# Cached attention on one Trainium2 core: K's transpose in two halves, the first wq on ScalarE's queue, K and V in whole transfers

## The chip, the cores and the metric

The kernel runs on one core of a Trainium2 chip. The metric is the time of one execution on the device in microseconds (us); the median of three runs stands for a kernel. A core has TensorE (PE, matrix products; its weight loads are shown apart as PEld), VectorE (DVE), ScalarE (ACT), GpSimd (POOL) and SyncE (SP), each with a program of its own. They meet through semaphores only. Transfers between the chip's main memory and the on-chip memory are issued by an engine and carried out by DMA engines. TensorE writes to eight banks of an accumulator memory called `ps` here.

## What is computed

Two independent attention blocks, A and B, whose results stand side by side in the output. For each:

```python
B, Sq, D = 16, 64, 640          # x: [B, Sq, D]
H, Sk, Dh = 32, 512, 128        # k_cache, v_cache: [B, H, Sk, Dh]
q = (x @ wq).reshape(B, Sq, H, Dh).transpose(0, 2, 1, 3)
scores = einsum("bhqd,bhkd->bhqk", q, k_cache) * Dh ** -0.5
p = softmax(scores, axis=-1)
o = einsum("bhqk,bhkd->bhqd", p, v_cache)
out = o.transpose(0, 2, 1, 3).reshape(B, Sq, H * Dh) @ wo
```

All inputs and the output are bf16. K and V are read once and are nearly all of the bytes.

## The kernel before

**Tiling.** The unit of work is a *pack* n: two batch rows (2 x 64 queries) and four heads. There are 128 packs. Four packs in a row (j = 0 to 3) share the two batch rows and make a group; eight groups make a phase, which uses one part of wq and wo (16 heads). Two phases do block A, two do block B. A pack needs 1 MB of K and 1 MB of V.

**Steps of a pack**, by the names that the plan uses:

- QP (L688): TensorE projects x to q, 20 matmuls. QE (L694): ScalarE copies q out of `ps`, scaled.
- KT (L702): VectorE transposes the pack's K, `kn_ring` to `kt_ring`, in one instruction of 128 x 2048 values of 4 bytes (pairs of bf16).
- S (L712): TensorE makes the scores, 32 matmuls in four accumulation steps f = 0 to 3. The steps f = 0, 1 read the half of K's transpose with index j = 0 in `kt_ring`, f = 2, 3 the half with j = 1.
- EX (L741): ScalarE takes the exponential of each of the four heads and its row sums; RC (L754): VectorE takes reciprocals, two heads at a time; NM (L762): GpSimd normalises P.
- TR (L774): TensorE transposes P; TE (L854): VectorE copies transposed P out of `ps`, in two instructions.
- PV (L867): TensorE multiplies P with V; OE (L875), ZO (L879): ScalarE copies the result out and clears the bank.
- OP (L887): TensorE multiplies with wo, accumulating over four packs; OS (L897, L900): VectorE adds the groups of two phases.

Beside these, per group: XT (L662), XE (L668), XS (L672), XC (L677) transpose and place x. Per phase: WP (L656), eight copies by GpSimd, permutes wq from `ws_sb`, where it lands, to `wqp_sb`, where QP reads it. A WP of pack 0 needs all five parts of wq (LDWQ, 512 KB each, in rows of 4 KB).

**Order.** `build_plan` writes out the order. Each step has a time in packs in the table `AT`; the program of each compute engine is its steps sorted by n plus that time. So TensorE runs S(n), TR(n-1), OP(n-2), QP(n+1), PV(n-1), S(n+1), and VectorE runs KT(n+1), TE(n-1), RC(n), KT(n+2). Before S(0) TensorE runs QP(0) and a dummy PV on zeros, n = -2. VectorE begins with memsets (VZ, BZ, WZ). TensorE's program and ScalarE's are loops of four packs; the first turn's instructions have to be brought in as it runs.

**Transfers.** SyncE issues nearly all of them, on one queue, in the order of a second key: LDWQ of the first phase at -50, then LDK(n), LDX, LDV(n) and LDWO by due time. At the start this gives five LDWQ, K(0), K(1), K(2), x of group 1, V(0), wo, K(3), V(1), wo, K(4), V(2) and so on. ScalarE's queue has one transfer, the first x. `kn_ring` holds six packs of K, `v_ring` four of V, `kt_ring` two transposes. LDV(n) may be issued when PV(n-4) is done, for which SyncE waits for TR(n-3). For packs below `KSPLIT` = 8, K comes in four transfers of 256 KB (L629) and V in two of 512 KB (L646); after that K comes in two of 512 KB (L631) and V in one of 1 MB (L641), but for the last two packs, whose V is cut otherwise (L648).

**Waits.** `stand_in` replaces a wait on a step by one on a later step that implies it, and `order_waits` drops those already implied. A step's wait for V or wo may stand with an earlier step of another engine.

Of the kernel before, what the change touches and what calls it, by code (L numbers as in the profile page):

```python
# [6 lines left out]
F32 = mybir.dt.float32  # L7
# [13 lines left out]
class Cfg:  # L21
    NK = 6
    NV = 4
    NKT = 2
# [5 lines left out]
    PERIOD = 4  # L30
    BASE = 32
    KLEAD = 2.5
    KSPLIT = 8
    NARROW = 2
    AFTER = 24
    AT = dict(XT=-2.585, XE=-2.383, XS=-1.65, XC=-0.788, QP=-0.428, QE=-0.224, KT=-0.672, S=0,
              EX=(0.307, 0.252, 0.358, 0.4), RC=(0.45, 0.6), RCO=0.48, NM=(0.803, 0.854, 1.088, 1.187),
              RCZ=(0.475, 0.6), NMZ=(0.48, 0.49, 0.61, 0.62), TR=1.293, TE=(1.432, 1.47), PV=1.701, OE=(1.888, 2.013), ZO=2.221,
              OP=2.387, OS=2.576, LDWO=2.6, ST=2.8,
# [47 lines left out]
def build_plan(dims, cfg, general):  # L87
# [4 lines left out]
    NPH, NBP, NJ = dims["NPH"], dims["NBP"], dims["NJ"]  # L92
    PH = NBP * NJ
    N = NPH * PH
    AT = cfg.AT
    ops = []
    loads = []
    at = {}

    def add(eng, kind, idx, ts, reads=(), writes=()):  # L100
        op = Op(eng, kind, idx, ts, reads, writes)
        ops.append(op)
        at[(kind, idx)] = op
        return op

    def add_output(n):
        g, j = n // NJ, n % NJ
        final = n >= 0 and dims["FINAL"](g // NBP)
        apart = 0 <= n < cfg.KSPLIT or n >= N - cfg.NARROW
        for b in range(0 if apart else 1, 2):  # L110
# [61 lines left out]
    for ph in range(NPH):  # L172
        twp = [ph * PH + t for t in AT["WP1" if ph else "WP0"]]
        for kt in range(dims["KT"]):
            ready = (twp[-1] - PH if ph > 1 else AT["WP0"][-1]) + 0.5
            op = add("sp", "LDWQ", (ph, kt), twp[0] - 0.5 if ph else -20.0, [], [("ws", kt, j) for j in range(NJ)])
            loads.append((ready + 2.0 + 0.14 * PH * kt if ph > 1 else AT["PV"] + 0.15 if ph else -50.0, 1, op))
        for j in range(NJ):
            w = ph * NJ + j
            n0 = ph * PH + j  # L180
            for i in range(2):
                add("pool", "WP", (w, i), twp[2 * j + i], [("ws", kt, j) for kt in range(dims["KT"])], [("wqp", j, i)])
            if ph:
                loads.append((n0 - NJ + AT["LDWO"], 4, add("sp", "LDWO", w, n0 + AT["OP"] - 0.8 * NJ, [], [("wo", j)])))
            else:
                loads.append((n0 - 1.9, 4, add("sp", "LDWO", w, n0 + AT["OP"] - 0.8 * NJ, [], [("wo", j)])))
# [6 lines left out]
    for n in range(-2, N):  # L193
        add_output(n)
        if n < 0:
            continue
        g, j = n // NJ, n % NJ
        add("pe", "QP", n, n + AT["QP"], [("xT", g % cfg.NX), ("wqp", j, 0), ("wqp", j, 1)], [("SB", 1)])
        add("act", "QE", n, n + AT["QE"], [], [("SB", 1), ("qs", n % cfg.NQ)])
        for i in range(4):  # L200
            if i < 2 or n < cfg.KSPLIT:
                op = add("sp", "LDK", (n, i), n + AT["KT"] - 0.9, [], [("kn", n % cfg.NK)])
                loads.append((n - cfg.NV + AT["PV"] + 0.2 - cfg.KLEAD, 2, op))
        add("dve", "KT", n, n + AT["KT"], [("kn", n % cfg.NK)], [("kt", n % cfg.NKT)])
        add("pe", "S", n, n + AT["S"], [("qs", n % cfg.NQ), ("kt", n % cfg.NKT)],
            [("SB", i) for i in range(4)])
        for i in range(4):
            h = 4 * n + i
            te = n + AT["EX"][i]
            if general:  # L210
                add("dve", "MX", h, te - 0.002, [], [("SB", i), ("negmax", h % 4)])
            add("act", "EX", h, te, [("negmax", h % 4)] if general else [],
                [("SB", i), ("pn", n % cfg.NPN, i), ("rs", n % cfg.NRS, i)])
            add("pool" if n < N - 1 else "dve", "NM", h, n + (AT["NM"] if n < N - 1 else AT["NMZ"])[i],
                [("recip", n, i // 2)], [("pn", n % cfg.NPN, i)])
        for a in range(2):
            add("dve", "RC", (n, a), n + (AT["RCZ"][a] if n == N - 1 else AT["RCO"] if n % NJ == 1 and not a else AT["RC"][a]), [("rs", n % cfg.NRS, i) for i in (2 * a, 2 * a + 1)],
                [("recip", n, a)])
# [62 lines left out]
    def stand_in(d, op):  # L281
        if op.eng == "pe":
            if d.kind == "XE":
                return at[("QE", max(0, NJ * d.idx - 2))]
            if d.kind == "NM" and d.eng == "pool":
                return at[("NM", d.idx | 3)]
            if d.kind == "OE":
                return d if d.idx[1] == 0 else at[("ZO", d.idx[0])]
            if d.kind in ("EX", "MX") and not for_pe(d):
                if op.kind == "S":  # L290
                    return at[("QE", op.idx)]
                return d if id(op) not in inside and d.kind == "EX" else None
            return d
        if d.kind == "PV" and op.eng == "sp":
            return at[("TR", d.idx + 1)]
        if d.kind == "QP" and op.eng == "pool":
            return at[("TR", d.idx - 1)]
        if d.kind == "XT" and op.eng == "sp":
            return at[("XE", d.idx)]
        if d.kind == "OS" and op.eng == "sp" and for_pe(d):  # L300
            return at[("RC", (d.idx * NJ + NJ + 1, 1))]
        if not for_pe(d):
            return d
        if d.kind == "NM":
            return at[("TR", d.idx // 4)]
        if d.kind == "KT":
            return at[("S", d.idx)]
        if d.kind == "EX":
            alt = at[("EX", d.idx // 4 * 4)]
            return at[("EX", d.idx // 4 * 4 + 2)] if for_pe(alt) else alt  # L310
        if d.kind == "OS":
            return at[("PV", d.idx * NJ + NJ)]
        if d.kind == "TE":
            return at[("PV", d.idx[0])]
        if d.kind == "OE":
            return at[("OP", d.idx[0])]
        if d.kind == "QE":
            return at[("S", d.idx)]
        if d.kind == "XC":
            return at[("QP", d.idx * NJ)]  # L320
        raise RuntimeError(f"no stand-in for {d.kind} before {op.kind}")
# [2 lines left out]
    counts = dict(base)  # L324

    def sem_key(op):
        if op.kind == "LDX" and op.eng == "act":
            return ("d_first",) + op.writes[0]
        if op.kind == "LDV":
            return ("d_v" if op.idx[1] else "d_vh", op.writes[0][1])  # L330
        if op.kind in LOADS:
            return ("d_" + op.kind[2:].lower(),) + op.writes[0][1:]
        if op.kind in ("ST", "STH"):
            return ("d_out",)
        return ("q_" + op.eng,) if for_pe(op) else ("s_" + op.kind.lower() + "_" + op.eng,)
# [169 lines left out]
def mha_kernel(nc, blocks, out, cfg=None):  # L505
    cfg = cfg or Cfg()
# [4 lines left out]
    KT = D // 128  # L511
    scale = float(DH) ** -0.5
    assert D // 2 + 128 <= 512
    NBP, NJ = B // 2, 4
# [15 lines left out]
    NK, NV, NKT, NX, NXN, NQ, NPN, NRS = (cfg.NK, cfg.NV, cfg.NKT, cfg.NX, cfg.NXN, cfg.NQ, cfg.NPN, cfg.NRS)  # L530

    with contextlib.ExitStack() as es:
# [8 lines left out]
        kn_ring = sb("kn_ring", [128, NK, 2, 2048], BF16)  # L541
        kt_ring = sb("kt_ring", [128, NKT, 32, 2, 2, 16, 2], BF16)
# [81 lines left out]
        def em_LDK(e, op):  # L624
            n, b, l = op.idx[0], op.idx[1] // 2, op.idx[1] % 2
            blk, bp, j, h = pack_info(n)
            src = blocks[blk][1][2 * bp:2 * bp + 2, h:h + 4].rearrange("b h (p l t) d -> l (h p) b (t d)", l=2, t=32)[l]
            if n < cfg.KSPLIT:
                ins = e.dma_start(kn_ring[2 * b + l::4, n % NK].rearrange("p a c -> p (a c)"), src[:, b])  # L629
# [66 lines left out]
            return ins, ins  # L696

        def em_KT(e, op):
            n = op.idx
            dst = kt_ring[:, n % NKT].rearrange("p t j b k two -> p (t j) b (k two)").bitcast(F32)  # L700
            src = kn_ring[:, n % NK].rearrange("p a c -> p (a c)").bitcast(F32).rearrange("p (c h b l) -> p c h b l", h=8, b=2, l=2)
            ins = e.transpose(dst.rearrange("p c b (h l) -> p c h b l", h=8, l=2), src)  # L702
            return ins, ins

        def em_S(e, op):
            n = op.idx
            first = last = None
            for f in range(4):
                for b in range(2):
                    for i in range(4):  # L710
                        rows = slice(32 * i, 32 * i + 32)
                        last = e.matmul(ps[64 * b:64 * b + 64, i, :], qs_ring[rows, n % NQ, f, b, :],  # L712
                                        kt_ring[rows, n % NKT, :, f // 2, b, :, f % 2],
                                        start=(f == 0), stop=(f == 3), tile_position=(32 * i, 64 * b))
                        first = first or last
            return first, last
# [354 lines left out]
```

## Time and profile before

The three runs took 731.67, 732.18 and 732.88 us, a median of 732.18. All views are of one profiled execution:

| what | value |
|---|---|
| time of the profiled execution | 732.12 us |
| its span, first to last instruction | 730.4 us |
| mean granted clock of TensorE | 0.99 |
| bytes moved by DMA | 295.02 MB, mean 404 GB/s |
| chain that ended last, shares | PE 53%, DMA 32%, SP's queue 6%, DVE 3% |
| VectorE's wait for K, both blocks | 120.4 us |
| TensorE's first projection | 15.48 us |

In the page's lists a row names line, engine, operation and tiles, then count, busy time, mean of one, and the idle time just before it with what ended it. In the 40 slices each digit is a share in tenths. The timeline gives start, duration, engine, line and tile, and in brackets how long the engine sat idle before it and for whom. A trailing q at an engine's name (SPq, ACTq) stands for its queue of transfers. "issue" marks idle time of an engine for which the profile shows no other engine or transfer as the reason.

### The profile page before, as it was taken

To read this page: it belongs to the slowest core of one execution; us is meant where nothing else is said; L and a number is where in the kernel's file an instruction comes from. 1 tells how busy PE (TensorE), PEld (TensorE's weight loads), DVE (VectorE), ACT (ScalarE), POOL (GpSimd) and SP (SyncE) were. 2 spreads that over 40 slices of the span, in tenths; PEclk is the share of its full clock that TensorE was granted. 3 is DMA by queue.
4 is the path that set the end of the run, shared out by engine and by line. 5 is a ranking of instruction groups with operands and counts; after the bars stand their busy time and mean duration, and the time that the engine had idled before them with its cause. 6 is when DMAs were issued, how large, how long until landed. Compare 5 with 4: busy or idle time off the path is not lost.

```text
span 730.4 us, 61195 instructions
## 1 busy us (share of the span) xinstructions
PE 674.1 (92%) x28502; PEld 530.3 (73%) x28502; DVE 514.5 (70%) x691; ACT 533.3 (73%) x1574; POOL 417.9 (57%) x596
## 2 busy tenths in 40 slices
PE   1679999999999999999997899999999799999998
PEld 1458778787777777777775677787777577787775
DVE  5447777777777766767765667677777567878775
ACT  1447878778787777777875677777778677878775
POOL 4436565666875455554884555465587446555552
PEclk9889999999999999999999999999999999999999
DMA  8999999999999999999999999999999999999993
GB/s 337 401 404 414 414 415 413 415 414 415 415 400 409 419 414 416 416 416 417 416 411 402 415 414 413 414 415 415 414 416 407 403 415 418 417 418 417 416 415 122
DMA packets 72336, 295.02 MB, mean 404 GB/s; under 512 B 7664, under 2 KB 20080, under 8 KB 55920
## 3 DMA queue, kind: packets, MB, share of 16 engines
q1 hardware_dynamic: 72160, 294.52, 100.0%
q8 instruction: 10, 0.16, 0.1%
q10 hardware_dynamic: 144, 0.16, 0.1%
q14 instruction: 22, 0.18, 0.1%
HBM read 292.03 MB, written 2.62 MB: 403 GB/s over the span
## 4 chain that ended last, share of the span: by engine, by line
PE 53%; DMA 32%; SPq 6%; DVE 3%; issue 3%; POOL 2%; ACT 1%; DVEq 0%; POOLq 0%
DMA xn_ring<-in_B_x_dram 14%; PE ps L867 12%; PE ps L887 11%; PE ps L688 11%; PE ps L712 10%; DMA kn_ring<-in_A_k_cache_dram 9%; PE ps L774 7%; DMA kn_ring<-in_B_k_cache_dram 5%; DMA wo_sb<-in_B_wo_dram 4%; SPq L631 4%; DVE kt_ring L702 2%; POOL pn_ring L762 2%; SPq L641 1%; DVE pT_sb L854 1%; SPq L615 1%
## 5 line engine op out<-in xcount | busy, mean ns | idle before, releaser
L762 POOL TENSOR_SCALAR pn_ring<-pn_ring,recip 128x512 bf16<-128x512 bf16 x508 | 343.4, 695 | 246.1 <-DVE recip L754 221.0
L702 DVE STREAM_TRANSPOSE kt_ring<-kn_ring 128x2048 f32<-128x2048 f32 x128 | 295.3, 2307 | 120.3 <-DMA kn_ring<-in_B_k_cache_dram 80.3
L741 ACT ACTIVATE pn_ring<-ps 128x512 bf16<-128x512 f32 x512 | 296.4, 592 | 5.7 <-PE ps L712 5.7
L854 DVE COPY pT_sb<-ps 128x1024 bf16<-128x1024 bf16 x256 | 168.4, 671 | 60.2 <-PE ps L774 60.2
L688 PE MATMUL ps<-xT_ring,wqp_sb 128*128 128x128 bf16 x2560 | 165.9, 220 | 11.6 <-POOL xT_ring L677 11.6
L867 PE MATMUL ps<-pT_sb,v_ring 32*128 32x64 bf16 x16448 | 162.2, 192 | 10.6 <-DVE pT_sb L854 4.6
L688 PEld LDWEIGHTS ps<-xT_ring,wqp_sb 128*128 128x128 bf16 x2560 | 157.5, 114 | 17.8 <-issue 11.8
L867 PEld LDWEIGHTS ps<-pT_sb,v_ring 32*128 32x128 bf16 x16448 | 147.0, 91 | 24.8 <-issue 12.5
L887 PE MATMUL ps<-wo_sb,oT_sb 128*128 128x320 bf16 x1024 | 163.5, 303 | 0.0
L875 ACT ACTIVATE oT_sb<-ps 128x256 bf16<-128x256 f32 x257 | 84.7, 381 | 95.1 <-PE ps L867 95.1
L712 PE MATMUL ps<-kt_ring,qs_ring 32*64 32x512 bf16 x4096 | 138.4, 380 | 4.8 <-issue 4.8
L694 ACT ACTIVATE qs_ring<-ps 128x512 bf16<-128x512 f32 x128 | 76.4, 597 | 76.5 <-PE ps L688 74.5
L774 PEld LDWEIGHTS ps<-ident,pn_ring 64*128 64x128 bf16 x4096 | 68.3, 95 | 77.0 <-ACT oT_sb L875 46.0
L887 PEld LDWEIGHTS ps<-wo_sb,oT_sb 128*128 128x128 bf16 x1024 | 90.4, 98 | 36.7
L741 ACT ACTIVATION_READ_ACCUMULATOR pn_ring<-ps 128x1 f32 x512 | 105.3, 206 | 0.0
L774 PE MATMUL ps<-ident,pn_ring 64*128 64x64 bf16 x4096 | 82.9, 191 | 22.8 <-POOL pn_ring L762 18.6
L712 PEld LDWEIGHTS ps<-kt_ring,qs_ring 32*64 32x64 bf16 x4096 | 53.4, 103 | 32.9 <-issue 5.5
L754 DVE RECIPROCAL recip<-rowsum 128x2 f32<-128x2 f32 x256 | 40.6, 158 | 27.6 <-ACT pn_ring L741 24.6
L879 ACT ACTIVATE ps<-zeros 128x256 f32<-128x256 bf16 x128 | 49.5, 387 | 4.1
L656 POOL COPY wqp_sb<-ws_sb 128x1280 bf16<-128x1280 bf16 x32 | 39.6, 1256 | 9.9 <-DMA ws_sb<-in_A_wq_dram 6.8
L668 ACT ACTIVATE xe_sb<-ps 128x640 bf16<-128x640 bf16 x32 | 22.9, 716 | 8.7 <-PE ps L662 8.6
L677 POOL COPY xT_ring<-xe_sb 128x640 bf16<-128x640 bf16 x16 | 11.5, 717 | 21.0 <-PE ps L774 21.0
(42 smaller groups left out, 103.5 us busy)
## 6 DMA issues: line engine op xcount, KB each, us to landing
kn_ring<-in_B_k_cache_dram SPq DMA_DIRECT2D x128, 512.0 KB, 16.1
v_ring<-in_B_v_cache_dram SPq DMA_DIRECT2D x62, 1024.0 KB, 16.5
kn_ring<-in_A_k_cache_dram SPq DMA_DIRECT2D x112, 512.0 KB, 11.4
v_ring<-in_A_v_cache_dram SPq DMA_DIRECT2D x56, 1024.0 KB, 14.8
kn_ring<-in_A_k_cache_dram SPq DMA_DIRECT2D x32, 256.0 KB, 8.6
v_ring<-in_A_v_cache_dram SPq DMA_DIRECT2D x16, 512.0 KB, 8.9
ws_sb<-in_A_wq_dram SPq DMA_DIRECT2D x10, 512.0 KB, 9.3
wo_sb<-in_A_wo_dram SPq DMA_DIRECT2D x8, 640.0 KB, 13.3
```

The costliest lines, as they stand in the source:

```text
L688: last = e.matmul(ps[:, 1, f * 128:(f + 1) * 128], w[:, kt, f, :], xT_ring[:, xs, kt, :], start=(kt == 0), stop=(kt == KT - 1))
L694: ins = e.activation(qs_ring[:, op.idx % NQ].rearrange("p f b q -> p (f b q)"), ps[:, 1, :], ACTF.Copy, scale=scale)
L702: ins = e.transpose(dst.rearrange("p c b (h l) -> p c h b l", h=8, l=2), src)
L712: last = e.matmul(ps[64 * b:64 * b + 64, i, :], qs_ring[rows, n % NQ, f, b, :], kt_ring[rows, n % NKT, :, f // 2, b, :, f % 2], start=(f = ...
L741: ins = e.activation(dst, src, ACTF.Exp, scale=1.0, accum_out=sum_of(h))
L762: ins = e.tensor_scalar(pn_view(h), pn_view(h), recip[:, h:h + 1], 1.0, ALU.mult, ALU.mult)
L774: last = e.transpose(pt_bank(b)[:, 64 * c:64 * c + 64], pn[rows, c, :], ident[rows, rows], tile_position=(64 * b, 0))
L854: ins = e.tensor_copy(pT_sb[:, b].rearrange("p t q -> p (t q)"), pt_bank(b))
L867: last = e.matmul(ps[:, 4 + i, 64 * b:64 * b + 64], v_ring[rows, n % NV, b, c, :], pT_sb[rows, b, c, :], start=(t == 0 and i < 2), stop=(t ...
L875: ins = e.activation(oT_sb[:, 2 * a:2 * a + 2, :], o_ps[:, 2 * a:2 * a + 2, :], ACTF.Copy)
L879: ins = e.activation(z_ps, zeros[:, :].unsqueeze(2).broadcast_to([128, 2, 128]), ACTF.Copy)
L887: last = e.matmul(out_ps[:, s, :], oT_sb[:, i, :], wo_sb[:, 4 * j + i, s * NH0:(s + 1) * NH0], start=(j == 0 and i == 0), stop=(j == NJ - ...
```

## The change

Three things are changed.

K's transpose and the scores are each made in two halves. `KT` becomes (n, 0) and (n, 1), each 128 x 1024 values; the second is placed at n - 0.39, which on VectorE is behind TE of pack n - 2 and the second RC of pack n - 1. The scores become S (f = 0, 1), which waits for the first half, and SL (f = 2, 3), which waits for the second and stands right behind S. The stand-ins for KT and QE become SL.

The first phase's five LDWQ are issued by ScalarE behind its load of x, with semaphores of their own (`d_first`); SyncE's queue begins with K(0).

`KSPLIT` becomes 0: K and V of the first eight packs come in the same transfers as those of later packs.

```diff
-    KSPLIT = 8
+    KSPLIT = 0
-    AT = dict(XT=-2.585, XE=-2.383, XS=-1.65, XC=-0.788, QP=-0.428, QE=-0.224, KT=-0.672, S=0,
+    AT = dict(XT=-2.585, XE=-2.383, XS=-1.65, XC=-0.788, QP=-0.428, QE=-0.224, KT=(-0.672, -0.39), SL=0.1, S=0,
...
-            op = add("sp", "LDWQ", (ph, kt), twp[0] - 0.5 if ph else -20.0, [], [("ws", kt, j) for j in range(NJ)])
-            loads.append((ready + 2.0 + 0.14 * PH * kt if ph > 1 else AT["PV"] + 0.15 if ph else -50.0, 1, op))
+            op = add("sp" if ph else "act", "LDWQ", (ph, kt), twp[0] - 0.5 if ph else -20.0 + 0.1 * kt, [],
+                     [("ws", kt, j) for j in range(NJ)])
+            if ph:
+                loads.append((ready + 2.0 + 0.14 * PH * kt if ph > 1 else AT["PV"] + 0.15, 1, op))
...
-                op = add("sp", "LDK", (n, i), n + AT["KT"] - 0.9, [], [("kn", n % cfg.NK)])
+                op = add("sp", "LDK", (n, i), n + AT["KT"][0] - 0.9, [], [("kn", n % cfg.NK)])
...
-        add("dve", "KT", n, n + AT["KT"], [("kn", n % cfg.NK)], [("kt", n % cfg.NKT)])
-        add("pe", "S", n, n + AT["S"], [("qs", n % cfg.NQ), ("kt", n % cfg.NKT)],
-            [("SB", i) for i in range(4)])
+        for a in range(2):
+            add("dve", "KT", (n, a), n + AT["KT"][a], [("kn", n % cfg.NK)], [("kt", n % cfg.NKT, a)])
+        add("pe", "S", n, n + AT["S"], [("qs", n % cfg.NQ), ("kt", n % cfg.NKT, 0)], [("SB", i) for i in range(4)])
+        add("pe", "SL", n, n + AT["SL"], [("qs", n % cfg.NQ), ("kt", n % cfg.NKT, 1)], [("SB", i) for i in range(4)])
...
-            return at[("S", d.idx)]
+            return at[("SL", d.idx[0])]
...
-            return at[("S", d.idx)]
+            return at[("SL", d.idx)]
...
-        if op.kind == "LDX" and op.eng == "act":
+        if op.kind in ("LDX", "LDWQ") and op.eng == "act":
...
-            n = op.idx
-            dst = kt_ring[:, n % NKT].rearrange("p t j b k two -> p (t j) b (k two)").bitcast(F32)
-            src = kn_ring[:, n % NK].rearrange("p a c -> p (a c)").bitcast(F32).rearrange("p (c h b l) -> p c h b l", h=8, b=2, l=2)
-            ins = e.transpose(dst.rearrange("p c b (h l) -> p c h b l", h=8, l=2), src)
+            n, a = op.idx
+            dst = kt_ring[:, n % NKT, :, a].rearrange("p t b k two -> p t b (k two)").bitcast(F32)
+            src = kn_ring[:, n % NK].rearrange("p a c -> p (a c)").bitcast(F32)
+            src = src.rearrange("p (t j h b l) -> p j t h b l", j=2, h=8, b=2, l=2)[:, a]
+            ins = e.transpose(dst.rearrange("p t b (h l) -> p t h b l", h=8, l=2), src)
             return ins, ins
 
         def em_S(e, op):
-            n = op.idx
+            return scores(e, op.idx, 0)
+
+        def em_SL(e, op):
+            return scores(e, op.idx, 2)
+
+        def scores(e, n, low):
             first = last = None
-            for f in range(4):
+            for f in range(low, low + 2):
```

## The prediction

> **What bounds the kernel now.** I read the page first (busy shares, the 40 slices, the chain), then cut the start into 1 us and 4 us windows, then the timeline of the start and of the end, and last what SyncE's queue waits for.
>
> ```profile
> span 730.4 us, 61195 instructions
> PE 674.1 (92%) x28502; PEld 530.3 (73%) x28502; DVE 514.5 (70%) x691; ACT 533.3 (73%) x1574; POOL 417.9 (57%) x596
> DMA  8999999999999999999999999999999999999993
> GB/s 337 401 404 414 414 415 413 415 414 415 415 400 409 419 414 416 416 416 417 416 411 402 415 414 413 414 415 415 414 416 407 403 415 418 417 418 417 416 415 122
> DMA packets 72336, 295.02 MB, mean 404 GB/s; under 512 B 7664, under 2 KB 20080, under 8 KB 55920
> L702 DVE STREAM_TRANSPOSE kt_ring<-kn_ring 128x2048 f32<-128x2048 f32 x128 | 295.3, 2307 | 120.3 <-DMA kn_ring<-in_B_k_cache_dram 80.3
> ```
>
> No engine is the bound, the transfers are: 295.02 MB at the 415 GB/s of the middle slices are 711 us of 730.4, and DMA share stays at 9 up to the last slice. Only the first slice (337 GB/s) and the last have room. TensorE is close behind. Where it is continuous (60 to 200 us) four packs of output projections (L887) go from 63.82 to 84.29, 5.12 us a pack; a pack's 2.10 MB of K and V with its share of x (0.04 MB) takes 5.15 us at 415 GB/s. So neither can make up time for the other: a microsecond in which the transfers run dry is lost for good.
>
> The start, in the timeline (start, duration, instruction, idle before it):
>
> ```profile
> 0.79 0.39 ACTq L608 DMA_DIRECT2D xn_ring<-in_A_x_dram  x1
> 0.93 2.39 SPq L615 DMA_DIRECT2D ws_sb<-in_A_wq_dram  x5
> 3.37 8.96 SPq L629 DMA_DIRECT2D kn_ring<-in_A_k_cache_dram  x12
> 12.22 2.45 POOL L656 COPY wqp_sb<-ws_sb 128x1280 bf16<-128x1280 bf16 x2 [6.80 <-DMA ws_sb<-in_A_wq_dram]
> 14.83 2.31 DVE L702 STREAM_TRANSPOSE kt_ring<-kn_ring 128x2048 f32<-128x2048 f32 x1 [4.74 <-DMA kn_ring<-in_A_k_cache_dram]
> 15.48 2.29 PE L688 MATMUL ps<-xT_ring,wqp_sb 128*128 128x128 bf16 x20 [11.58 <-POOL xT_ring L677]
> 18.38 1.78 PE L867 MATMUL ps<-pT_sb,v_ring 32*128 32x64 bf16 x128 [0.60 <-DVE pT_sb L852]
> 32.37 1.49 PE L712 MATMUL ps<-kt_ring,qs_ring 32*64 32x512 bf16 x19 [4.81 <-issue]
> 34.85 0.82 SPq L646 DMA_DIRECT2D v_ring<-in_A_v_cache_dram  x2
> 58.90 0.81 SPq L646 DMA_DIRECT2D v_ring<-in_A_v_cache_dram  x2
> ```
>
> TensorE's first projection waits for wq (landed about 12.1), then GpSimd's two permuting copies (2.45) and the copy of x (0.72). And from 34.85 on each V is issued only once TensorE has reached the next transposes of P:
>
> ```profile
> SPq L641 <- PE ps L774: 251.1, 105, 4.5
> SPq L646 <- PE ps L774: 17.5, 5, 4.9
> ```
>
> So TensorE's clock drives the transfers, with a cover: what is issued and not yet landed. Adding the GB/s of 1 us windows, 22.53 MB have moved by 58.90; issued by then (summed over the program) are 24.08. That is 1.55 MB, 3.7 us; at 34.85 (12.79 of 14.35 MB), 53.81 and 63.93 the same sum gives 3.7 to 3.8. A new transfer's first bytes come about 1.1 us after its issue (0.79 to some 1.9, the first window with traffic), so **the cover is 2.65 us** of TensorE lateness.
>
> **The change, part by part.**
>
> *wq on ScalarE's queue.* Five issues at the 0.39 to 0.48 us of SyncE's rows, 2.2 us, stand before ScalarE's table load (1.28) and the first x copy (3.94), which becomes about 4.7; x is next needed at 14.6, so nothing. SyncE starts K(0) at 0.93, not 3.37. It is then past the second x load by about 6 (not 12.38; it waits for the x copy) and has V(0), V(1) and two parts of wo queued by about 10, where V(1) had been issued at 17.06. What matters is that wq now shares the engines with K from the first byte. Nothing in the trace shows two large queues side by side, so bounds: if wq lost nothing, it lands at 12.1 as now. If the queues share bytes equally, 2 x 2.62 + 0.16 MB must move where 2.79 sufficed; the windows reach 5.41 MB at 16.4 us, less the 1.0 gained below, plus the 1.85 between 2.79 MB moved (10.25) and the landing: 17.3, **5.2 later**. If they alternate row by row, K's 8 KB rows take two bytes for wq's one: K(0) to K(2), 3.15 MB, beside 1.57 of wq, then V's equal rows beside the other 1.05, in all 6.98 MB, which the windows reach at 20.3: 21.1, 9.0 later. All that follows shifts with it, except that the dummy P x V no longer waits 0.60 for VectorE, which finishes K(0) and its memsets early: 4.6 or 8.4 at the first scores. I take **5.5**, a quarter of the way, since transfers of 512 KB meet transfers of 512 KB but with longer rows in K's.
>
> By the Trainium skill (DMA: Bandwidth & Descriptors, "Issuing engines are not separate DMA queues"), transfers of all queues run on the same 16 engines and interleave, so a second queue saves only issue time; the same page's "Queues, rings and completion order" has each engine alternate between queues packet by packet. By that rule the lossless bound is out and the late start is 4.6 or more, a sum of at least +1.15; by the trace, in which only the 160 KB of x ran on ScalarE's queue (2.3 us to landing), it stays possible. It speaks against this part of the change.
>
> *K and V whole.* 72336 less 55920 packets are 16416 of 8 KB or more; K's rows are 128 x 128 = 16384, so K moves in 8 KB rows cut or whole, and bytes and packets stay. SyncE's work falls: 12 issues took 8.96 us, 0.75 per 256 KB, or 351 GB/s, below what the engines move. In the 1 us windows traffic is 238 GB/s from 6 to 7, where this bites, and about 255 from 2 to 4. Filling 2 to 9 us at 410 would bring 0.65 MB, 1.6 us; a first ramp stays, so between 0 and 1.6, and I take **1.0 us earlier transfers**. It only counts if TensorE does not hold the transfers up later: with a late TensorE it merely makes them run dry sooner.
>
> *K's transpose in halves.* VectorE takes 2307 ns for 2048 columns. Half the columns are 1154 ns at least; fixed cost is bounded by its smallest row, the reciprocal of 2 columns at 158 ns, so 1154 to 1312, and I take 1.23 (half of 2307 - 158, plus 158). That is 0.15 a pack more on an engine 70% busy. The copies of transposed P no longer stand behind 2.31 but 1.23 when K is late, so P x V may start 1.08 earlier after a landing. Near the end K sets the pace again and again:
>
> ```profile
> 604.83 2.31 DVE L702 STREAM_TRANSPOSE kt_ring<-kn_ring 128x2048 f32<-128x2048 f32 x1 [1.30 <-DMA kn_ring<-in_B_k_cache_dram]
> 609.25 1.21 PE L867 MATMUL ps<-pT_sb,v_ring 32*128 32x64 bf16 x128 [0.23 <-DVE out_sb L900]
> 712.74 2.31 DVE L702 STREAM_TRANSPOSE kt_ring<-kn_ring 128x2048 f32<-128x2048 f32 x1 [0.86 <-DMA kn_ring<-in_B_k_cache_dram]
> ```
>
> From 609 TensorE runs on without a gap worth naming, in step with K (20 transposes in 102.5 us, 5.13 each). With 1.08 less behind each landing it can pass this stretch earlier by 0.23 (its idle there) to 1.08 (all of it, from idle between 580 and 600). I take **0.8 gained**. Between 225 and 600 the saturated transfers hide any gain.
>
> The second half is queued behind the second reciprocal, which waits for ScalarE's last exponential. Around 703: scores end 703.93, that reciprocal 706.46 to 706.63, half two ends 707.86, and the low scores start at about 708.4 (scores of the next pack at 707.88 plus half of 1.07). Slack 0.5 us, so no cost. If that cover were gone, 0.1 us a pack would cost 2.3 us over the last 23 packs. Queued behind the half are only the next pack's transpose and copies, over 1 us later. The extra wait on TensorE goes to the same queue order: transposes of P behind it need the normalised P, ready later than K.
>
> **Sum.** Late start 5.5, less cover 2.65: transfers end 2.85 later; less 0.8 at the end: +2.05. On the profiled execution's 732.12 (span 730.4 and 1.7 around it; median 732.18) that is **734.2**. TensorE's instruction stalls at 24 to 45 us (1.64, 4.81, 3.98) are kept as they are; after two of them its clock is 0.5 for about 6 us.
>
> **Rivals.** (1) *The start is covered, and the kernel is faster.* If wq keeps most of its pace, or the stalls shrink because fewer bytes are in flight (4.81 under the 3 us after which the clock fell at 30.4 would save some 2 and another 3 of slow clock), TensorE is late by less than 2.65 - 1.0 = 1.65 us, which is the point that decides; then -1.0 - 0.8 = -1.8: 730.3. For it: the stalls are the larger part of the start. Against: wq cannot have two thirds of the traffic and K too. (2) *A draw.* Equal sharing and stalls 1.2 shorter: 4.6 - 1.2 - 2.65 - 0.8 = 0: 732.1. (3) *Row by row sharing.* 8.4 - 2.65 - 0.8 = +4.95: 737.1. For it: K's rows are twice wq's. (4) *The second half comes late in each pack*, by 0.1 beyond its slack: 2.3 more than the forecast, 736.5; against it the 0.5 us counted above.
>
> **How the numbers follow.** Forecast 0.36, (1) 0.28, (2) 0.22, (3) 0.11, (4) 0.03. A measurement of this kernel tells 0.2% (1.5 us) from no change. Faster 0.28, same 0.22, slower 0.50. The range goes from 729.8 (rival 1 with all of 1.08 and 1.3 of the start) to 737.3. The forecast's own: 733.0 to 735.8.
>
> **What would show it.** First projection near 20 instead of 15.48, GpSimd's first copies waiting for wq until 17 to 18; DMA share below 0.9 in windows somewhere between 25 and 60 us, SyncE waiting longer for L774 there; transposes of K of 1.23 us, and no TensorE wait for the second half. I am wrong if wq lands before 14, or if DMA share stays full through the start although TensorE begins late.

## The result, and the profile after

The changed kernel took 739.43 us, the median of four runs (738.38 to 740.0); the kernel before took 732.26 beside it. The ratio is 1.0099, with a 95% interval from 1.0086 to 1.0111: 7.2 us slower. The profiled execution took 740.0 us, with a span of 738.3.

The page of the changed kernel: the totals, the traffic in 40 slices of 18.5 us, the queues, and the transposes of K.

```profile
span 738.3 us, 61291 instructions
PE 676.3 (92%) x28502; PEld 531.7 (72%) x28502; DVE 530.8 (72%) x819; ACT 533.4 (72%) x1574; POOL 417.8 (57%) x596
GB/s 339 401 282 391 392 415 413 414 414 416 416 406 404 416 414 417 415 417 415 417 415 401 411 415 413 415 414 415 413 416 408 402 415 418 415 418 418 416 414 116
q1 hardware_dynamic: 71056, 291.89, 98.3%
q10 hardware_dynamic: 864, 2.79, 1.0%
L706 DVE STREAM_TRANSPOSE kt_ring<-kn_ring 128x1024 f32<-128x1024 f32 x256 | 310.4, 1228 | 61.8 <-DMA kn_ring<-in_B_k_cache_dram 33.3
```

The work is the same but for the halves on VectorE, and from the sixth slice on the traffic is what it was. The third slice fell from 404 to 282 GB/s, the next two from 414 to 391 and 392. So the loss is made in the first five slices, 92 us.

The start, in the timeline:

```profile
1.21 3.25 ACTq L618 DMA_DIRECT2D ws_sb<-in_A_wq_dram  x5
20.29 2.45 POOL L659 COPY wqp_sb<-ws_sb 128x1280 bf16<-128x1280 bf16 x2 [13.02 <-DMA ws_sb<-in_A_wq_dram]
23.55 2.29 PE L691 MATMUL ps<-xT_ring,wqp_sb 128*128 128x128 bf16 x20 [19.60 <-POOL xT_ring L680]
39.88 1.49 PE L721 MATMUL ps<-kt_ring,qs_ring 32*64 32x512 bf16 x19 [4.81 <-issue]
42.37 0.37 SPq L644 DMA_DIRECT2D v_ring<-in_A_v_cache_dram  x1
```

wq lands at 20.2 instead of 12.1, TensorE begins at 23.55 instead of 15.48, and V(3) is issued at 42.37 instead of 34.85. The same stall of 4.81 comes with it. What this does to the transfers stands in windows of 1 us; the columns behind the engines' busy times are TensorE's granted clock, DMA share and GB/s:

```profile
37.00:38.00 1.00, 0.00 (x0) 0.00 (x0) 0.00 (x0) 0.00 (x0) 0.00 (x0) 0.50 1.05 418
38.00:39.00 1.00, 0.00 (x0) 0.00 (x0) 0.00 (x0) 0.00 (x0) 0.00 (x0) 0.50 0.55 213
39.00:40.00 1.00, 0.12 (x8) 0.12 (x15) 0.00 (x0) 0.00 (x0) 0.00 (x0) 0.50 0.20 82
40.00:41.00 1.00, 1.00 (x19) 0.31 (x18) 0.00 (x0) 0.00 (x0) 0.00 (x0) 0.50 0.00 0
41.00:42.00 1.00, 1.00 (x31) 0.70 (x30) 0.00 (x0) 0.58 (x2) 0.00 (x0) 0.50 0.06 16
42.00:43.00 1.00, 1.00 (x17) 0.61 (x12) 0.62 (x2) 1.00 (x5) 0.00 (x0) 0.50 0.00 0
43.00:44.00 1.00, 1.00 (x5) 0.61 (x4) 0.74 (x3) 0.84 (x4) 0.16 (x1) 0.50 0.77 82
44.00:45.00 1.00, 1.00 (x9) 0.77 (x8) 0.37 (x1) 0.00 (x0) 1.00 (x2) 0.50 0.81 242
45.00:46.00 1.00, 1.00 (x15) 1.00 (x13) 1.00 (x3) 0.70 (x1) 0.58 (x2) 0.62 1.06 430
```

In the kernel before the same stretch is full:

```profile
39.00:40.00 1.00, 1.00 (x93) 0.85 (x101) 1.00 (x1) 0.10 (x1) 1.00 (x2) 1.00 1.04 422
42.00:43.00 1.00, 0.00 (x0) 0.00 (x0) 0.00 (x0) 1.00 (x5) 0.00 (x0) 1.00 1.14 401
```

After the change the transfers run dry. Two things are to be seen. They fade over 2 us (213, 82) instead of stopping, and after V(3) is issued at 42.37 they need until 45 to be back at full rate.

Adding the GB/s of windows of 20 us gives the bytes moved at a time; their difference, divided by 415 GB/s, is how far the transfers are behind the kernel before. How late TensorE is, is read from the starts of the same output projection (L887 before, L896 after), the one nearest to that time in the kernel before. Turns of TensorE's program are counted by the n of its S(n); turn n runs the output projection of pack n - 2:

| | 20 us | 40 | 60 | 80 | 100 | 300 | 500 | 700 | end of the loop |
|---|---|---|---|---|---|---|---|---|---|
| MB moved before | 6.86 | 14.86 | 22.98 | 31.26 | 39.54 | 122.24 | 204.92 | 287.80 | |
| MB moved after | 6.90 | 14.42 | 20.78 | 28.30 | 36.52 | 119.16 | 201.82 | 284.64 | |
| transfers behind, us | -0.1 | 1.1 | 5.3 | 7.1 | 7.3 | 7.4 | 7.5 | 7.6 | |
| TensorE late, us | | 7.5 | 8.3 | 8.3 | 8.3 | 7.8 | 8.1 | 8.1 | 8.1 |

By 80 us nearly the whole loss is there (7.1 of transfers, 8.3 of TensorE), and it is never recovered. That is the reading of the profile before, that neither can make up time for the other.

### The profile page after: what moved, and what is told of

Same layout as the page of the kernel before. It is cut to its first block, busy times and chain, and to the rows that moved or that the text cites. A ratio compares the mean times of both kernels' runs of the same rounds, so it can differ in the third digit from the quotient of the medians.

```text
span 738.3 us, 61291 instructions
## 1 busy us (share of the span) xinstructions
PE 676.3 (92%) x28502; PEld 531.7 (72%) x28502; DVE 530.8 (72%) x819; ACT 533.4 (72%) x1574; POOL 417.8 (57%) x596
## 3 DMA queue, kind: packets, MB, share of 16 engines
HBM read 292.03 MB, written 2.62 MB: 399 GB/s over the span
## 4 chain that ended last, share of the span: by engine, by line
PE 58%; DMA 30%; SPq 5%; issue 2%; POOL 2%; ACT 1%; DVE 1%; ACTq 0%; DVEq 0%; POOLq 0%
DMA xn_ring<-in_B_x_dram 14%; PE ps L876 13%; PE ps L896 13%; PE ps L691 12%; PE ps L721 11%; PE ps L783 7%; DMA v_ring<-in_A_v_cache_dram 5%; DMA wo_sb<-in_B_wo_dram 4%; SPq L634 4%; DMA kn_ring<-in_A_k_cache_dram 3%; DMA v_ring<-in_B_v_cache_dram 2%; DMA ws_sb<-in_A_wq_dram 2%; POOL pn_ring L771 1%; SPq L644 1%; PE ps L665 1%
## 5 line engine op out<-in xcount | busy, mean ns | idle before, releaser
L706 DVE STREAM_TRANSPOSE kt_ring<-kn_ring 128x1024 f32<-128x1024 f32 x256 | 310.4, 1228 | 61.8 <-DMA kn_ring<-in_B_k_cache_dram 33.3
L863 DVE COPY pT_sb<-ps 128x1024 bf16<-128x1024 bf16 x256 | 170.6, 678 | 101.3 <-PE ps L783 100.6
L896 PE MATMUL ps<-wo_sb,oT_sb 128*128 128x320 bf16 x1024 | 164.5, 304 | 0.0
L896 PEld LDWEIGHTS ps<-wo_sb,oT_sb 128*128 128x128 bf16 x1024 | 90.7, 99 | 37.2
## 6 DMA issues: line engine op xcount, KB each, us to landing
v_ring<-in_B_v_cache_dram SPq DMA_DIRECT2D x62, 1024.0 KB, 16.8
ws_sb<-in_B_wq_dram SPq DMA_DIRECT2D x10, 512.0 KB, 18.2
```

The lines of the kernel that those rows point to most:

```text
L706: ins = e.transpose(dst.rearrange("p t b (h l) -> p t h b l", h=8, l=2), src)
L863: ins = e.tensor_copy(pT_sb[:, b].rearrange("p t q -> p (t q)"), pt_bank(b))
L896: last = e.matmul(out_ps[:, s, :], oT_sb[:, i, :], wo_sb[:, 4 * j + i, s * NH0:(s + 1) * NH0], start=(j == 0 and i == 0), stop=(j == NJ - ...
```

## The experiments

Times are medians beside runs of the kernel before on the same chip. Each was predicted by a theory in which a late wq is all, against rivals named with it.

**One part undone, or one part alone.** Four kernels take the change apart. In the first, the first wq is back on SyncE's queue:

```diff
-            op = add("sp" if ph else "act", "LDWQ", (ph, kt), twp[0] - 0.5 if ph else -20.0 + 0.1 * kt, [],
+            op = add("sp", "LDWQ", (ph, kt), twp[0] - 0.5 if ph else -20.0, [], [("ws", kt, j) for j in range(NJ)])
...
```

> The changed kernel with the first wq back on SyncE's queue ahead of K; halves and whole transfers stay. Late wq is all (my theory): the first projection is back near 15.5 us, DMA share stays full between 38 and 45 us, and the time is 730.5 to 732.5, that is at least 6.5 of the 7.2 us come back. Rival, the whole transfers of the first eight packs cost (fewer, larger pieces, so each lands later): wq lands near 12 again but the time stays above 735. Rival, the half transposes cost: above 734 with TensorE waiting in the middle of the scores or behind wo.

Measured: 732.05 against 732.01, ratio 0.9995 (0.9986 to 1.0004). The first projection starts at 15.40, and the whole loss is gone with this one part undone. The second kernel is the one before with that part alone:

> The kernel before with nothing but the first wq moved to ScalarE's queue; K in four transfers of 256 KB, its transpose whole. My theory: wq lands at 18 to 20.5, the first projection starts at 21.5 to 24 and the time is 737 to 740. If the whole transfers or the halves make the loss, it is 732 to 734. SyncE's slow issue of cut K (351 GB/s) could leave wq more of the traffic: then wq lands near 17 and the time is near 736.

Measured: 738.64, ratio 1.0080 (1.0066 to 1.0094), so this part alone costs 6.6 of the 7.2 us; the rest lies within the intervals of the two ratios. wq lands at 19.7:

```profile
19.79 2.45 POOL L658 COPY wqp_sb<-ws_sb 128x1280 bf16<-128x1280 bf16 x2 [12.64 <-DMA ws_sb<-in_A_wq_dram]
23.05 2.29 PE L690 MATMUL ps<-xT_ring,wqp_sb 128*128 128x128 bf16 x20 [19.15 <-POOL xT_ring L679]
```

The third has the whole transfers alone:

```diff
-    KSPLIT = 8
+    KSPLIT = 0
```

> The kernel before with nothing but K and V of the first eight packs in whole transfers. By the gain that I took for it (1.0 us of earlier transfers): 731.2. If the transfers are not ahead at 20 us, as in the changed kernel: 732.2 within 0.7. If the whole transfers are what costs: 735 or more.

Measured: 731.93, ratio 0.9999 (0.9990 to 1.0008). Neither the gain nor a cost: at 20 us its transfers are 0.2 us ahead (6.94 MB against 6.86). The fourth has the half transposes and half scores alone:

> The kernel before with nothing but the transposes of K and the scores in halves. By the prediction's term: 0.8 faster, 731.4, with TensorE about 1 us nearer to K's landings. If the packs that wait for wo take the lead back (TensorE's lateness against the kernel before returns at packs 67 and 99): 732.2 within 0.5. If the second half behind the reciprocals costs: 733 or more, with TensorE idle before the second part of the scores.

Measured: 731.88, ratio 0.9998 (0.9989 to 1.0007). TensorE leads the kernel before by 0.84 us up to turn 36 and by 0.9 to 1.7 in turns 41 to 49, is 0.6 late at turn 68, 2.0 to 2.2 in turns 70 to 72 and 0.9 in turns 98 to 103, and ends its loop 0.03 late. In turns 98 to 101 GpSimd's last normalising copy of a pack also waits for wo, and TensorE's transposes wait for it. The last of these waits in the kernel before (first line) and in this one:

```profile
583.77 0.69 POOL L762 TENSOR_SCALAR pn_ring<-pn_ring,recip 128x512 bf16<-128x512 bf16 x1 [2.45 <-DMA wo_sb<-in_B_wo_dram]
584.69 0.69 POOL L769 TENSOR_SCALAR pn_ring<-pn_ring,recip 128x512 bf16<-128x512 bf16 x1 [2.44 <-DMA wo_sb<-in_B_wo_dram]
585.53 0.64 PE L781 MATMUL ps<-ident,pn_ring 64*128 64x64 bf16 x32 [1.61 <-POOL pn_ring L769]
```

wo lands 0.9 later here, so TensorE comes out of these waits 0.9 late. Behind them the kernel before still idles 0.44 us at 598.50 and 0.23 at 609.25; this one has no idle time over 0.15 us from 585.53 to 721, and so comes level. The gain behind K is there, but it only makes up for the late wo. K and V land later too. The time from issue to landing of V between 600 and 700 us, before and here, and the transpose of K that starts at 712.74 in the kernel before:

```profile
v_ring<-in_B_v_cache_dram SPq DMA_DIRECT2D x20, 1024.0 KB, 15.9
v_ring<-in_B_v_cache_dram SPq DMA_DIRECT2D x20, 1024.0 KB, 16.8
713.78 1.25 DVE L704 STREAM_TRANSPOSE kt_ring<-kn_ring 128x1024 f32<-128x1024 f32 x1 [0.73 <-DMA kn_ring<-in_B_k_cache_dram]
```

The first kernel, which has the halves, shows 16.8 as well, and the third, which has not, 16.0. As many bytes have moved (287.82 MB by 700 us against 287.80), so why the landings come later stays open, and no run took the waits for wo away.

**How much lateness is covered.** Here nothing of the change is made. GpSimd repeats the first copy of wq, two or five times, so that TensorE starts late and every queue is as before:

```diff
+    for i in range(2):
+        add("pool", "HD", i, -1.2 + 0.01 * i, [("ws", kt, 0) for kt in range(dims["KT"])], [("wqp", 0, 0)])
...
+        def em_HD(e, op):
+            return em_WP(e, Op("pool", "WP", (0, 0), 0.0))
```

> The kernel before, with GpSimd repeating the first permuting copy of wq twice, 2 x 1.25 us, so that TensorE's first projection starts 2.5 us later and nothing else changes; the dummy P x V no longer waits 0.60, so TensorE is 1.9 late. By the cover of the prediction (2.65): no loss, 732.0. By the cover that the changed kernel shows (TensorE 8.28 late, transfers 7.3 late: 1.0): 0.9 lost, 732.9. If the loss comes from two queues side by side and not from the late start: 732.0.

> The same with five repeats, 6.25 us: TensorE is 5.65 late. By a cover of 2.65: 735.0. By a cover of 1.0: 736.7. If two queues side by side make the loss: 732. If a late TensorE finds its instructions sooner (shorter stalls): 734 or less, with stalls well below 4.81 and 3.98.

Measured: 733.55, ratio 1.0018 (1.0009 to 1.0027), and 737.30, ratio 1.0076 (1.0064 to 1.0088). Two queues side by side are not needed for the loss; a late TensorE alone makes it. Both times contradict a cover of 2.65 and stand at or above the 732.9 and 736.7 of a cover of 1.0. In the profiled executions, which are 0.6 us shorter than the medians, TensorE came out 1.5 and 4.9 late, 0.4 and 0.7 less than expected; the stalls shrank a little (1.1, 4.4 and 3.0 us in the second, not 1.6, 4.8 and 4.0), far from the rival. In the second kernel the transfers run dry just as after the change:

```profile
21.97 2.30 PE L693 MATMUL ps<-xT_ring,wqp_sb 128*128 128x128 bf16 x20 [18.12 <-POOL xT_ring L682]
38.00:39.00 1.00, 1.00 (x19) 0.23 (x3) 0.00 (x0) 0.00 (x0) 0.00 (x0) 0.50 0.55 221
39.00:40.00 1.00, 1.00 (x35) 0.81 (x32) 0.00 (x0) 0.70 (x3) 0.00 (x0) 0.50 0.20 82
40.00:41.00 1.00, 1.00 (x14) 0.56 (x9) 0.66 (x2) 1.00 (x4) 0.00 (x0) 0.50 0.00 0
```

**How two queues share.** The changed kernel, with K of the first three packs in rows half as long:

```diff
+            if n < 3:
+                ins = e.dma_start(kn_ring[l::2, n % NK, b], kv[l])
...
```

> The changed kernel, with K of the first three packs in four transfers of 256 KB with rows of 4 KB instead of two with rows of 8 KB; the same bytes on the same queue. If the two queues take turns row by row, wq's 4 KB rows now get half instead of a third: wq lands near 17.3 instead of 20.2, and the time falls by some 2.9 to 736.5. If they share by transfers or by bytes, wq lands at 20 and the time stays at 739. The finer issues cost SyncE time too (twelve at 0.5 to 0.75 us), which would help wq in either case by 1 us at most.

Measured: 737.69, ratio 1.0081 (1.0065 to 1.0096), a loss of 5.7 us instead of 7.2; wq landed at 18.8. The intervals of the two ratios touch, but the transfers are 4.1 us behind at 100 us instead of 7.3. The sign fits turns by row, the size is 1.5 short of 17.3: 0.3 MB less had moved by 20 us (6.60, not 6.90), which is 0.7. The rest may lie in the end of wq: by 16 us all but 0.08 of its 2.62 MB had moved, and the last row only by 18.2. The queues themselves show the turns. Packets, MB and share of the two queues from 8 to 10 us, first of the changed kernel with its packets by size, then of this one:

```profile
DMA packets 162, 0.82 MB, mean 410 GB/s; under 512 B 28, under 2 KB 28, under 8 KB 96
q1 hardware_dynamic: 80, 0.53, 65.6%
q10 hardware_dynamic: 81, 0.28, 35.7%
```

```profile
q10 hardware_dynamic: 121, 0.44, 54.6%
q1 hardware_dynamic: 113, 0.37, 46.6%
```

SyncE's queue (q1) and ScalarE's (q10) move as many packets each, 80 and 81. 28 of these are 4 bytes long; the others are 65 of K's rows of 8 KB and 68 of wq's rows of 4 KB: two bytes of K for one of wq. With rows of equal length the bytes come out near equal. By the Trainium skill (DMA: Bandwidth & Descriptors, "Queues, rings and completion order") each engine alternates between queues at packet granularity, a packet being typically 9 to 17 descriptors. The trace agrees that the queues alternate, with 65 rows against 68. It shows no turns of whole transfers: both queues carry transfers of 512 KB here, which would share bytes equally, and in the second kernel, where K comes in transfers half as large, the packets from 8 to 10 us are 89 against 85 as well.

**wq over both queues.** Parts 0, 2 and 4 by ScalarE, 1 and 3 by SyncE ahead of K:

```diff
-            op = add("sp" if ph else "act", "LDWQ", (ph, kt), twp[0] - 0.5 if ph else -20.0 + 0.1 * kt, [],
+            op = add("act" if not ph and kt % 2 == 0 else "sp", "LDWQ", (ph, kt), twp[0] - 0.5 if ph else -20.0 + 0.1 * kt, [],
...
```

> The changed kernel with the first wq cut over both queues, parts 0, 2, 4 by ScalarE and 1, 3 by SyncE ahead of K. Late wq as the cause says: wq's last part meets only K(0) for a short time, lands at 12 to 13.5, the first projection starts at 15.5 to 17, and the time is 731.5 to 733. If any K beside wq is as bad as all of it: above 735.

Measured: 733.79, ratio 1.0026 (1.0017 to 1.0035); wq at 14.9, the first projection at 18.19, TensorE 1.3 late from turn 5 on. Later than expected, and the time is above the range I gave: SyncE is done with its two parts early (the second landed at 10.05), and the last of ScalarE's three then shares with K until 13 us.

**K held back.** The changed kernel, in which SyncE's first K waits for the third part of wq:

```diff
+    at[("LDK", (0, 0))].deps.append(at[("LDWQ", (0, 2))])
```

> The changed kernel, wq still on ScalarE's queue, but SyncE's first K waits until the third of the five parts of wq has landed; nothing else moves. If sharing the engines with K is what makes wq late, and not the queue that it is on: wq lands between 12 and 14.5, no or few packets of SyncE's queue before 8 us, the first projection starts at 15.3 to 18, and the time is 731.5 to 733.5. If ScalarE's queue itself is slow: wq still lands at 17 or later and the time is above 736.

Measured: 734.60, ratio 1.0036 (1.0022 to 1.0050). wq alone lands at 12.7 on ScalarE's queue, TensorE starts at 15.97 and is even 0.8 earlier than before from turn 4 to turn 32; so the queue is not slow, the sharing is. But the time missed my range, by a price that I had left out:

```profile
10.19 3.85 SPq L636 DMA_DIRECT2D kn_ring<-in_A_k_cache_dram  x6
10.00:11.00 1.00, 0.00 (x0) 0.00 (x0) 0.09 (x1) 0.00 (x0) 0.00 (x0) 1.00 0.56 225
11.00:12.00 1.00, 0.00 (x0) 0.00 (x0) 0.00 (x0) 0.00 (x0) 0.00 (x0) 1.00 0.41 131
```

The third part of wq lands only at 10.2, and between wq's last bytes and K's first the traffic falls to 225 and 131 GB/s. By 20 us 1.12 MB less have moved, 2.7 us at 415 GB/s, and 2.7 is the loss. TensorE is early for 32 turns, is 2.3 late from turn 37, and the kernel is slow all the same: the transfers decide.

TensorE's steady lateness from turn 5 to 30, the transfers behind at 100 us (MB not yet moved, by 415 GB/s), and how much longer the span of the same profiled execution is, side by side:

| kernel | TensorE late | transfers behind | covered | span against before | median against before |
|---|---|---|---|---|---|
| wq over both queues | 1.29 | 0.5 | 0.8 | +1.2 | +1.8 |
| held by 2.5 | 1.54 | 0.3 | 1.2 | +0.9 | +1.5 |
| K in 4 KB rows | 4.81 | 4.1 | 0.7 | +4.4 | +5.7 |
| held by 6.25 | 4.94 | 4.1 | 0.8 | +4.6 | +5.3 |
| wq on ScalarE alone | 7.27 | 6.3 | 1.0 | +6.9 | +6.6 |
| the change | 8.28 | 7.3 | 1.0 | +7.9 | +7.2 |

Five kernels, two with GpSimd held and three with wq late by different edits, lie near one line with the change: by the transfers about 1 us of lateness is covered, and each microsecond beyond it is a microsecond of transfers lost. By the spans still less is covered, 0.1 to 0.7. The medians stand 0.1 to 1.6 off the transfers of one profiled execution and are too coarse to tell 0.4 from 1.0; none leaves room for 2.65. So the size of the cover is known only as about 1 or less. No version beat the kernel before; the three that leave wq on SyncE's queue and hold nothing back are level with it.

## Why the prediction was wrong, step by step

**The bound** was right: the transfers bound the kernel, TensorE paces them through V's buffers, and lost time stays lost. All nine runs agree with that.

**The late start was mis-sized.** The prediction bounded it by 4.6 and 8.4 at the first scores and put it at 5.5, "a quarter of the way, since transfers of 512 KB meet transfers of 512 KB". The upper bound was the right mechanism: the queues take turns row by row, the size of a transfer plays no part (with K in transfers of 256 KB wq landed at 19.7, with 512 KB at 20.2, bound 21.1), the scores came 7.5 late, and TensorE ran 8.28 late after that, with a third stall 0.3 longer and the clock at 0.5 for 10.2 us, to 45.8, instead of 6.8. This is 2.8 of the miss, 2.0 of it at the first scores. The rival with row-by-row sharing, given 0.11, named the cause; nothing in the trace before could settle it, but K's packets of 8 KB and wq's of 4 KB were both in its rows.

**The cover was mis-sized.** 3.7 us of issued bytes less 1.1 to the first byte gave 2.65; by the transfers it is 0.7 to 1.2, by the spans 0.1 to 0.7. The windows from 38 to 45 us show what was left out: the backlog fades out at 213 and 82 GB/s in its last 2 us, with a DMA share of 0.55 and 0.20, and a single V brings the traffic back by steps (82, 242, 430). So full rate ends before the last byte has moved; that some of the engines run empty first fits the shares, but the profile does not show the engines one by one. An estimate from these windows: the fade costs 1.3 us at 415 GB/s, and from V(3)'s issue on 1.85 are missing instead of 1.1, so of 3.7 some 0.55 are left. With a cover of 1.0 this is 1.65 of the miss.

**The halves** cost and did what was said: 1228 ns each against an estimate of 1.23 us, with no wait of TensorE before the second half of the scores. The gain of 0.8 at the end is what failed. With the halves alone TensorE does win 0.9 behind turn 103, but it enters that stretch 0.9 late, because wo lands 0.9 later there, so 0 remains (ratio 0.9998). The prediction let the landings stay where they were; why they moved, those of K and V too, is open.

**The whole transfers** were put at 1.0 earlier transfers that would not count; there was next to nothing to count, 6.94 MB alone and 6.90 in the changed kernel against 6.86 at 20 us. The early gap that was put down to SyncE's slow issue stays with the whole transfers alone (229 GB/s from 6 to 7 us, 238 before); in the changed kernel others take its place, 246 from 4 to 5 and 307 and 348 from 11 to 13. V(1), said to be queued by about 10, was issued at 12.71.

**The stalls** of TensorE were kept as they are, nearly rightly: 1.13, 4.81 and 4.27 against 1.64, 4.81 and 3.98, and in the most held kernel still 1.1, 4.4 and 3.0. In both kernels each ends 1.3 to 1.6 us after a 16 KB packet on a queue of instructions (q8) has ended: before, the packet that ends at 30.91 and TensorE going on at 32.37.

With the measured terms the sum is 8.3 - 1.0 - 0 = 7.3, against 7.2. It has to come out near, since the 1.0 is read from the same kernel's 8.3 and 7.3; what tests it is that the other five kernels of the table give covers near it, 0.7 to 1.2.

## What to carry to other kernels

When the first thing that an engine needs shares the transfers with bulk data on a second queue, it does not get its turn by bytes: here rows took turns (65 against 68), and the shorter rows lost. Put what is needed first ahead of the rest on one queue, and count a backlog as cover only for as long as it keeps the full rate, which ended here some 2 us before it was used up. In a kernel bound by transfers, a shorter path on an engine gains nothing unless it keeps the transfers from running dry.

## What the runs showed of the hardware that was not expected

Two queues with work share packet for packet (80 to 81 in 2 us), so their bytes went by the length of their rows (0.53 to 0.28 MB). A wait between two queues in place of an order on one costs the time from a landing to the next first byte: the run in which K was held back was 2.7 us of traffic behind at 20 us. Cutting K and V of the first packs finer or coarser, at the same row length, made no difference (ratio 0.9999).
